# Moving the later forget-logit loads of a gated-attention and MLP-mixer kernel to the queue of its other loads, in the order of need

## The chip, the cores and the metric

The kernel runs on one core of a Trainium2 chip. The metric is device time in microseconds (us), lower is better. The planner inside the kernel, not the compiler, decides the order of instructions on each engine, so a small edit can change the order of many others. Engines: TensorE (PE) with its weight loads (PEld), VectorE (DVE), ScalarE (ACT), GpSimd (POOL) and SyncE (SP). POOL issues loads on the software queue, SP on the sync queue. A run counts as slow when it took over 1.5% longer than the fastest run of the same kernel; only the other, fast runs are compared.

## The reference, cut to what matters

```python
batch, n_heads, seq, head_dim = (4, 8, 768, 48)
f = 1.0 / (1.0 + np.exp(-f_logit))
for t in range(S):                                   # gated linear attention
    state = f[:, :, t, :, None] * state + einsum('bhd,bhe->bhde', k[:, :, t], v[:, :, t])
    y[:, :, t] = einsum('bhd,bhde->bhe', q[:, :, t], state)
x = y as (B, S, 384)
h = np.maximum(x.T @ w_tok1, 0.0) @ w_tok2           # token mixing, 768 -> 256 -> 768
u = x + h.T
out = u + np.maximum(u @ w_ch1, 0.0) @ w_ch2         # channel mixing, 384 -> 1536 -> 384
```

Inputs and output are float32. Each batch is cut into six chunks of 128 time steps. While a batch is mixed, the attention of the next one runs between its matmuls.

## The kernel before

Every load is a node of a plan: POOL, SP or DVE spends some time on it, then a made-up engine `Q` transfers it. The order of issue on each engine is all that the plan decides.

```python
    def load_f(b, c, key, at=0.0):                    # forget logits: sync queue, float32
        i = b % 2
        deps = [made.get(("lo", b - 2, c))]           # the buffer's last reader
        if b:
            def token(e):                             # holds the load back until DVE gets here
                nc.vector.memset(f_sb[i][0:1, c, 0, 0:1], 0.0)
            deps = [add({"DVE": 0.06}, token, key, deps, at=at)]
        def issue(e):
            nc.sync.dma_start(out=f_sb[i][:, c], in_=chunk_of(f_logit, b, c))
        n = add({"SP": 0.1}, issue, key, deps, at=at)
        made["f", b, c] = add({"Q": 1.1}, None, key, [n])

    def load_qkv(b, c, key, at=0.0):                  # software queue, cast to bfloat16
        ...
            made[name, b, c] = swdge(
                lambda e, dst=dst, src=src: nc.gpsimd.dma_start(out=dst[i][:, c], in_=chunk_of(src, b, c)), ...)

    def gates(b, c0, c1, key):                        # Exp, Ln -> Lhi, Ln, then Llo = f - Lhi
        ...
        o = add({"POOL": 0.85 * n} if b > 1 else {"DVE": 0.4 * n + 0.08},
                lambda e: on(e).tensor_tensor(lo, fb, hi, ALU.subtract), key, [g, h])
...
        xn = made["xn", b, c] = add(..., copy(e, x_nat[i][:, c, :], t["py"][:, 0:DM]))   # PSUM -> float32
        made["xb", b, c] = add(..., copy(e, x_bf[i][:, c, :], x_nat[i][:, c, :]))        # -> bfloat16
...
    for c in range(NCH):
        load_f(0, c, 0.1 * c)
        load_qkv(0, c, 0.1 * c)
    load_w("w_tok1", ...); load_w("w_tok2", ...); load_w("w_ch1", ...)
    for c in range(NCH):
        if c == W2:
            load_w("w_ch2", ...)
        load_f(1, c, 0.63 + 0.01 * c, at=24.0 + 2.0 * c + (6.0 if c >= W2 else 0.0))
        load_qkv(1, c, 0.63 + 0.01 * c)
    ...
                if b >= 1:
                    load_f(b + 1, c, b + 0.05 + 0.1 * c)       # no `at`: as soon as the buffer is free
                    load_qkv(b + 1, c, b + 0.05 + 0.1 * c)
```

`tok1`, `tok2`, `ch1`, `ch2` below are the matmuls with the four weights. Lhi is the logarithm of the forget gate (with its sign turned) in bfloat16, Llo what that rounding left over; attention needs both. x_bf is the attention's output in bfloat16, h1T the inner activation of token mixing.

## Time and profile before

| | before |
|---|---|
| median of 4 runs | 216.56 us (216.18 to 218.65) |
| span of the profiled run | 215.3 us |
| first tok2 / ch1 / ch2 matmul of batch 0 | 42.6 / 51.2 / 73.7 us |
| last packet of q/k/v of batches 0, 1, 2, 3 | 26.2 / 75.3 / 92.3 / 116.9 us |
| w_ch2 landed | 73.6 us |

Landings are from the packet records of the trace. From the page of the kernel before, busy time of each engine and the queues; a queue's line has packets, MB and the time of its packets as a share of the 16 DMA engines' span:

```profile
PE 182.8 (85%) x1768; PEld 112.8 (52%) x1768; DVE 134.7 (63%) x317; ACT 141.7 (66%) x315; POOL 77.5 (36%) x90
...
q0 software_dynamic: 77888, 10.23, 70.9%
q1 hardware_dynamic: 28416, 9.44, 25.1%
```

The busy times by stage, kernel before. Each line: stretch, its length, busy time of each engine (instructions), granted TensorE clock, DMA share (time of the packets over that of the 16 DMA engines; packets overlap, so it can exceed 1), GB/s:

```profile
0.00:20.00 20.00, 7.21 (x77) 4.28 (x78) 8.72 (x28) 11.44 (x25) 14.57 (x24) 1.00 1.61 133
20.00:40.00 20.00, 15.93 (x178) 10.28 (x177) 15.42 (x43) 14.90 (x35) 11.73 (x14) 1.00 1.63 173
40.00:60.00 20.00, 17.06 (x158) 9.81 (x159) 14.61 (x42) 15.35 (x38) 8.88 (x10) 0.83 1.75 136
60.00:80.00 20.00, 17.46 (x179) 10.94 (x178) 13.96 (x35) 13.89 (x35) 8.75 (x10) 0.91 1.71 156
80.00:110.00 30.00, 25.82 (x297) 15.93 (x296) 25.80 (x51) 23.05 (x49) 25.75 (x26) 0.94 1.73 125
```

PE is idle 16.9 us in the first 40 us. The chain of waits of the kernel before (start, length, what) shows why:

```profile
6.16 11.41 DMA v_sb_82<-in_v_dram
...
23.93 13.63 DMA w_ch_76<-in_moe_w_ch_dram
...
37.84 16.27 DMA k_sb_81<-in_k_dram
...
54.41 19.22 DMA w_ch_77<-in_moe_w_ch_dram
73.68 2.10 PE pm L452 x6
```

The chain goes from load to load until w_ch2 (w_ch_77) lands and lets PE start ch2. The issues on SP's queue (start, length, the load, buffer 84 for even batches, 85 for odd ones):

```profile
0.75 33.30 SPq L211 DMA_DIRECT2D f_sb_84<-in_f_logit_dram  x11
34.10 3.44 SPq L211 DMA_DIRECT2D f_sb_85<-in_f_logit_dram  x1
37.64 2.06 SPq L211 DMA_DIRECT2D f_sb_84<-in_f_logit_dram  x1
39.76 33.80 SPq L211 DMA_DIRECT2D f_sb_85<-in_f_logit_dram  x11
```

Buffer 84 gets six loads for batch 0 and six for batch 2, and all twelve are issued by 37.6 us. So five of the six loads of batch 2, which nothing reads before 79 us, were issued before the first load of batch 1.

### The profile page before, as it was taken

What the parts mean: (1) busy time and instruction counts of PE and PEld (TensorE: products, weight loads), DVE (VectorE), ACT (ScalarE), POOL (GpSimd) and SP (SyncE); (2) the same over time, 40 slices, a digit from 0 to 9 for tenths busy, and PEclk for the clock granted to TensorE, in tenths of its full rate; (3) what the DMA queues carried; (4) which work ended last, traced back from release to release, by engine and by line L of the source; (5) the groups of instructions that cost most, each with busy time, mean ns of one, the idle gap of its engine ahead of it and who ended that gap; (6) DMA issues with size and microseconds to landing.
All of it is one profiled execution on the core that took longest, in us unless ns stands there. A gap on an engine that the chain in (4) does not pass through costs nothing.

```text
span 215.3 us, 4558 instructions
## 1 busy us (share of the span) xinstructions
PE 182.8 (85%) x1768; PEld 112.8 (52%) x1768; DVE 134.7 (63%) x317; ACT 141.7 (66%) x315; POOL 77.5 (36%) x90
## 2 busy tenths in 40 slices
PE   0525789588999597978989999998999999899993
PEld 0313555354566264645555656665666665466661
DVE  4428795386999538798898544779566584620122
ACT  5646796576999267495999924478986442789200
POOL 8937960434543179998495300000000000000000
PEclk9999999976999889996999999999999999999999
DMA  7999999999999999999979002210000132000032
GB/s 114 146 135 139 152 204 188 134 135 135 137 151 184 146 139 182 113 79 139 133 66 75 3 35 74 76 38 3 0 3 0 37 106 82 2 3 0 0 142 81
DMA packets 106326, 19.96 MB, mean 93 GB/s; under 512 B 100288, under 2 KB 105920, under 8 KB 106304
## 3 DMA queue, kind: packets, MB, share of 16 engines
q0 software_dynamic: 77888, 10.23, 70.9%
q1 hardware_dynamic: 28416, 9.44, 25.1%
q8 instruction: 14, 0.23, 0.5%
q14 instruction: 8, 0.07, 0.1%
HBM read 25.17 MB, written 4.72 MB: 139 GB/s over the span
## 4 chain that ended last, share of the span: by engine, by line
PE 52%; DMA 28%; DVE 6%; ACT 5%; POOL 5%; issue 2%; DVEq 0%; POOLq 0%
PE pm L452 21%; PE pm L433 16%; DMA w_ch_77<-in_moe_w_ch_dram 9%; DMA k_sb_81<-in_k_dram 8%; DMA w_ch_76<-in_moe_w_ch_dram 6%; DMA v_sb_82<-in_v_dram 5%; PE pm L384 3%; POOL k_sb_80 L228 2%; PE pm L403 1%; DVE u_nat_118 L407 1%; POOL q_sb_78 L228 1%; POOL v_sb_82 L228 1%; PE pk L292 1%; PE pq L292 1%; ACT u_bf L189 1%
## 5 line engine op out<-in xcount | busy, mean ns | idle before, releaser
L452 PE MATMUL pm<-w_ch_77,zT 128*128 128x384 bf16 x288 | 53.3, 331 | 2.5 <-DMA w_ch_77<-in_moe_w_ch_dram 2.5
L433 PE MATMUL pm<-uT,w_ch_76 128*128 128x384 bf16 x288 | 53.0, 330 | 0.0
L195 ACT ACTIVATE zT<-pm 128x384 bf16<-128x384 f32 x78 | 37.9, 503 | 4.1 <-PE pm L433 3.8
L452 PEld LDWEIGHTS <-zT 128*128 128x128 bf16 x288 | 26.8, 99 | 19.4 <-DMA w_ch_77<-in_moe_w_ch_dram 2.6
L433 PEld LDWEIGHTS <-w_ch_76 128*128 128x128 bf16 x288 | 26.7, 98 | 16.1 <-issue 0.7
L461 DVE TENSOR_TENSOR out_sb_122<-u_nat_118,pm 128x384 f32<-128x384 f32 x6 | 3.3, 550 | 17.5 <-PE pm L452 17.4
L228 POOL DMA_DIRECT2D k_sb_80<-in_k_dram x12 | 10.7, 888 | 9.1 <-DMA w_ch_77<-in_moe_w_ch_dram 6.5
L228 POOL DMA_DIRECT2D k_sb_81<-in_k_dram x12 | 10.8, 898 | 8.7 <-DMA w_ch_76<-in_moe_w_ch_dram 5.3
L403 PE MATMUL pm<-h1T,w_tok_75 128*128 128x384 bf16 x48 | 11.9, 371 | 2.1 <-ACT uT L189 1.2
L228 POOL DMA_DIRECT2D v_sb_83<-in_v_dram x12 | 10.8, 903 | 5.7 <-DMA q_sb_79<-in_q_dram 4.2
L228 POOL DMA_DIRECT2D q_sb_79<-in_q_dram x12 | 10.9, 912 | 4.3 <-DMA k_sb_81<-in_k_dram 2.4
L228 POOL DMA_DIRECT2D q_sb_78<-in_q_dram x12 | 10.9, 906 | 3.7 <-DMA k_sb_80<-in_k_dram 1.3
L228 POOL DMA_DIRECT2D v_sb_82<-in_v_dram x12 | 10.7, 896 | 3.5 <-DMA q_sb_78<-in_q_dram 1.4
L197 DVE TENSOR_SCALAR zT<-pm 128x384 bf16<-128x384 f32 x18 | 9.6, 551 | 3.2 <-PE pm L433 3.0
L189 ACT COPY x_nat_112<-py 128x384 f32<-128x384 f32 x11 | 5.3, 478 | 9.3 <-PE py L352 8.5
L272 ACT ACTIVATE G_90<-pS 128x384 bf16<-128x384 f32 x12 | 6.0, 497 | 7.3 <-PE pS L266 7.3
L418 PE MATMUL pm<-ident,u_bf 128*128 128x128 bf16 x72 | 7.5, 223 | 2.1 <-DVE u_bf L191 0.6
L259 PE MATMUL pS<-Lhi_86,tri_bf 128*128 128x384 bf16 x12 | 5.0, 415 | 4.9 <-ACT Lhi_86 L243 4.9
L384 PEld LDWEIGHTS <-w_tok_74 128*128 128x128 bf16 x48 | 5.2, 114 | 7.4 <-issue 6.0
L272 ACT ACTIVATE G_91<-pS 128x384 bf16<-128x384 f32 x12 | 5.8, 488 | 4.9 <-PE pS L260 3.4
L189 ACT COPY x_nat_113<-py 128x384 f32<-128x384 f32 x9 | 4.4, 492 | 6.8 <-PE py L352 6.8
L407 DVE TENSOR_TENSOR u_nat_118<-x_nat_113,pm 128x384 f32<-128x384 f32 x12 | 6.1, 546 | 3.9 <-PE pm L403 3.9
(228 smaller groups left out, 422.4 us busy)
## 6 DMA issues: line engine op xcount, KB each, us to landing
f_sb_84<-in_f_logit_dram SPq DMA_DIRECT2D x12, 192.0 KB, 8.3
f_sb_85<-in_f_logit_dram SPq DMA_DIRECT2D x12, 192.0 KB, 9.0
out_dram<-out_sb_122 SPq DMA_DIRECT2D x12, 192.0 KB, 1.9
out_dram<-out_sb_123 SPq DMA_DIRECT2D x12, 192.0 KB, 2.0
q_sb_78<-in_q_dram POOLq DMA_DIRECT2D x12, 96.0 KB, 7.1
k_sb_80<-in_k_dram POOLq DMA_DIRECT2D x12, 96.0 KB, 6.7
v_sb_82<-in_v_dram POOLq DMA_DIRECT2D x12, 96.0 KB, 7.0
w_ch_76<-in_moe_w_ch_dram POOLq DMA_DIRECT2D x1, 1152.0 KB, 13.6
```

Of the source, the lines that this page charges most:

```text
L189: nc.scalar.copy(dst, src)
L195: nc.scalar.activation(dst, src, AF.Relu, bias=0.0, scale=1.0)
L197: nc.vector.tensor_scalar(dst, src, 0.0, None, ALU.max)
L228: lambda e, dst=dst, src=src: nc.gpsimd.dma_start(out=dst[i][:, c], in_=chunk_of(src, b, c)),
L259: nc.tensor.matmul(Sv, lhsT=tri_bf, rhs=Lhi[i][:, c, :, 0:D], start=True, stop=False)
L272: return lambda e: nc.scalar.activation(dst.rearrange("t h d -> t (h d)"), t["pS"][:, 0:DM], AF.Exp, bias=0.0, scale=scale)
L384: nc.tensor.matmul(t["p"][:, 0:DM], lhsT=w_tok1[:, kt, rt * 128:(rt + 1) * 128], rhs=x_bf[i][:, kt, :], start=(kt == 0), stop=(kt == NCH - 1))
L403: nc.tensor.matmul(t["p"][:, 0:DM], lhsT=w_tok2[:, kt, tt * 128:(tt + 1) * 128], rhs=h1T[:, kt, :], start=(kt == 0), stop=(kt == 1))
L407: u = made["u", b, tt] = add({"DVE": 0.47}, lambda e, tt=tt, t=t: nc.vector.tensor_tensor(u_nat[i][:, tt, :], x_nat[i][:, tt, :], t["p"][: ...
L418: nc.tensor.matmul(t["p"][:, m * 128:(m + 1) * 128], lhsT=u_bf[:, tt, m * 128:(m + 1) * 128], rhs=ident, start=True, stop=True)
L433: nc.tensor.matmul(t["p"][:, 0:384], lhsT=w_ch1[:, kt, cc * 128:(cc + 1) * 128], rhs=uT[:, kt, th * 384:(th + 1) * 384], start=(kt == 0), ...
L452: nc.tensor.matmul(t["p"][:, 0:DM], lhsT=zT[:, kt, tt * 128:(tt + 1) * 128], rhs=w_ch2[:, kt, :], start=(kt == 0), stop=(kt == NCC - 1))
```

## The change

The intent: loads of later batches off the sync queue, so that one queue carries all loads but the forget logits of batch 0, in the order in which they are needed; the first loads before the masks are built. With it came a re-tuning of the plan. The diff, cut to its core:

```diff
-    make_upper_triangular(nc, tri_bf, val=1.0, diag=True)
-    make_identity(nc, ident)
-    f_sb = two([128, NCH, H, D], FP32, "f_sb")
+    f_sb = two([128, H, NCH, D], FP32, "f_sb")
-    out_sb = two([128, DM], FP32, "out_sb")
+    out_sb = [st([128, DM], FP32, f"out_sb{n}") for n in range(NCH)]
...
+        if b == 0:
+            ... six loads on the sync queue, as before
+        else:
+            m = swdge(lambda e: nc.gpsimd.dma_start(out=f_sb[i], in_=src), key, 2.28, 5.9, 0.3,
+                      [made.get(("lo", b - 2, c)) for c in range(NCH)], at)
...
-        o = add({"POOL": 0.85 * n} if b > 1 else {"DVE": 0.4 * n + 0.08},
+        o = add({"POOL": 0.85 * n, "DVE": 0.4 * n + 0.08} if b > 1 else {"DVE": 0.4 * n + 0.08},
...
-        made["xb", b, c] = add(..., copy(e, x_bf[i][:, c, :], x_nat[i][:, c, :]), ...)
+        made["xb", b, c] = add(..., copy(e, x_bf[i][:, c, :], t["py"][:, 0:DM]), ...)
...
-    PACE = (34.0, 5.6)
+    PACE = (34.0, 5.0)
+    load_f(0, 0.0)
+    load_qkv(0, 0, 0.0)
+    def masks(e):
+        make_upper_triangular(nc, tri_bf, val=1.0, diag=True)
+        make_identity(nc, ident)
+    made["masks"] = add({"POOL": 1.4}, masks, 0.0)
+    ... q/k/v of batch 0, w_tok1, w_tok2
+    load_f(1, 0.615)
+    load_w("w_ch1", ...)
+    ... q/k/v of batch 1, w_ch2 before its last chunk
...
-            n = 2 if b else 1
+            n = 2
-                gates(b + 1, c, c + n, b + 0.9 + 0.15 * c)
+                gates(b + 1, c, c + n, b + 0.85 + LEAD[0] + LEAD[1] * c)
```

More of the change, by code (lines that the diff above doesn't have):

```diff
@@ L200, in chunk_of, with swdge, load_f @@
         return src[b].rearrange("h (c t) d -> t h c d", t=C)[:, :, c, :]
-    def load_f(b, c, key, at=0.0):
-        i = b % 2
-        deps = [made.get(("lo", b - 2, c))]
-        if b:
-            def token(e):
-                nc.vector.memset(f_sb[i][0:1, c, 0, 0:1], 0.0)
-            deps = [add({"DVE": 0.06}, token, key, deps, at=at)]
-        def issue(e):
-            nc.sync.dma_start(out=f_sb[i][:, c], in_=chunk_of(f_logit, b, c))
-        n = add({"SP": 0.1}, issue, key, deps, at=at)
-        made["f", b, c] = add({"Q": 1.1}, None, key, [n])
-    issued = []
-    def swdge(fn, key, cost, us, deps, at=0.0):
-        ring = [issued[-6]] if len(issued) >= 6 else []
+    issued = []
+    def swdge(fn, key, cost, us, units, deps, at=0.0):
+        room, ring = 6.5 - units, []
+        for m, u in reversed(issued):
+            room -= u
+            if room < 0:
+                ring = [m]
+                break
         n = add({"POOL": cost}, fn, key, list(deps) + ring, at=at)
         m = add({"Q": us}, None, key, [n])
-        issued.append(m)
+        issued.append((m, units))
         return m
+    def load_f(b, key, at=0.0):
+        i = b % 2
+        src = f_logit[b].rearrange("h (c t) d -> t h c d", t=C)
+        if b == 0:
+            for c in range(NCH):
+                n = add({"SP": 0.05}, lambda e, c=c: nc.sync.dma_start(out=f_sb[i][:, :, c, :], in_=src[:, :, c, :]),
+                        key, [])
+                made["f", b, c] = add({"Q": 1.1}, None, key + 0.06 * c, [n])
+        else:
+            m = swdge(lambda e: nc.gpsimd.dma_start(out=f_sb[i], in_=src), key, 2.28, 5.9, 0.3,
+                      [made.get(("lo", b - 2, c)) for c in range(NCH)], at)
+            for c in range(NCH):
+                made["f", b, c] = m
     def load_qkv(b, c, key, at=0.0):
@@ L228, in load_qkv, with load_w @@
                 lambda e, dst=dst, src=src: nc.gpsimd.dma_start(out=dst[i][:, c], in_=chunk_of(src, b, c)),
-                key, 0.89, 0.72, [made.get((u, b - 2, c)) for u in users], at)
-    def load_w(name, dst, src, key, us):
+                key, 0.89, 0.71, 1.0, [made.get((u, b - 2, c)) for u in users], at)
+    def load_w(name, dst, src, key, us, units):
         made[name] = swdge(
             lambda e: nc.gpsimd.dma_start(out=dst, in_=src.rearrange("(kt p) n -> p kt n", p=128)),
-            key, 0.85, us, [])
+            key, 0.85, us, units, [])
     def gates(b, c0, c1, key):
@@ L238, in gates @@
         cs = range(c0, c1)
-        fb, hi, lo = f_sb[i][:, c0:c1], Lhi[i][:, c0:c1, :, 0:D], Llo[i][:, c0:c1, :, 0:D]
+        fb = f_sb[i].rearrange("t h c d -> t c h d")[:, c0:c1]
+        hi, lo = Lhi[i][:, c0:c1, :, 0:D], Llo[i][:, c0:c1, :, 0:D]
         cost = 0.08 + 0.33 * n
@@ L268, in attention @@
                                     [made["lo", b, c], made.get(("qh", *p2)), made.get(("kh", *p2)),
-                                     made.get(("st", *p2))], bank="att", at=at)
+                                     made.get(("st", *p2)), made["masks"]], bank="att", at=at)
         def decay(dst, scale):
@@ L341, in diag @@
                 copy(e, state_bd[j][64:64 + D, :, D:2 * D], state[j][64:64 + D])
-            made["bd", b, c] = add({"DVE": 0.5, "ACT": 0.5}, diag, key + 0.02, [s_, made.get(("y", *p2))])
+            made["bd", b, c] = add({"DVE": 0.5, "ACT": 0.55}, diag, key + 0.02, [s_, made.get(("y", *p2))])
         def readout(e):
@@ L356, in attention @@
                                   ms + [made["v", b, c], made.get(("bd", b, c - 1)) if c else None], bank="att")
-        xn = made["xn", b, c] = add({"ACT": 0.38, "DVE": 0.47},
-                                    lambda e: copy(e, x_nat[i][:, c, :], t["py"][:, 0:DM]),
-                                    key + 0.03, [made.get(("u", b - 2, c))], frees=y)
-        made["xb", b, c] = add({"DVE": 0.28, "ACT": 0.4},
-                               lambda e: copy(e, x_bf[i][:, c, :], x_nat[i][:, c, :]),
-                               key + 0.03, [xn, made.get(("t1", b - 2))])
+        either = {"ACT": 0.38, "DVE": 0.47}
+        made["xb", b, c] = add(either, lambda e: copy(e, x_bf[i][:, c, :], t["py"][:, 0:DM]),
+                               key + 0.03, [made.get(("t1", b - 2))], frees=y)
+        made["xn", b, c] = add(either, lambda e: copy(e, x_nat[i][:, c, :], t["py"][:, 0:DM]),
+                               key + 0.03, [made.get(("u", b - 2, c))], frees=y)
     def mixing(b, key0, span):
@@ L408, in mixing @@
                 u_nat[i][:, tt, :], x_nat[i][:, tt, :], t["p"][:, 0:DM], ALU.add),
-                kk, [made.get(("o", b - 2, tt))], frees=n)
+                kk, [made["xn", b, tt], made.get(("o", b - 2, tt))], frees=n)
             ub = add({"DVE": 0.28, "ACT": 0.4},
@@ L459, in mixing @@
             made["c2", b, tt] = half
-            o = out_sb[tt % 2]
+            o = out_sb[tt]
             n = made["o", b, tt] = add({"DVE": 0.47}, lambda e, tt=tt, t=t, o=o: nc.vector.tensor_tensor(
                 o, u_nat[i][:, tt, :], t["p"][:, 0:DM], ALU.add),
-                kk, [half, made.get(("out", tt % 2))], frees=first)
+                kk, [half, made.get(("out", tt))], frees=first)
             s = add({"SP": 0.1}, lambda e, tt=tt, o=o: nc.sync.dma_start(out=out_b[tt], in_=o), kk, [n])
-            made["out", tt % 2] = add({"Q": 0.7}, None, kk, [s])
+            made["out", tt] = add({"Q": 0.7}, None, kk, [s])
     W2 = 5
-    PACE = (34.0, 5.6)
-    for c in range(NCH):
-        load_f(0, c, 0.1 * c)
+    LEAD = (-0.05, 0.13)
+    PACE = (34.0, 5.0)
[5 more added lines that the diff above has]
+    made["masks"] = add({"POOL": 1.4}, masks, 0.0)
+    for c in range(1, NCH):
         load_qkv(0, c, 0.1 * c)
-    load_w("w_tok1", w_tok1, moe_w_tok1, 0.60, 3.3)
-    load_w("w_tok2", w_tok2, moe_w_tok2, 0.61, 2.2)
-    load_w("w_ch1", w_ch1, moe_w_ch1, 0.62, 6.0)
+    load_w("w_tok1", w_tok1, moe_w_tok1, 0.60, 3.0, 0.75)
+    load_w("w_tok2", w_tok2, moe_w_tok2, 0.61, 2.2, 0.25)
+    load_f(1, 0.615)
+    load_w("w_ch1", w_ch1, moe_w_ch1, 0.62, 6.0, 0.4)
     for c in range(NCH):
         if c == W2:
-            load_w("w_ch2", w_ch2, moe_w_ch2, 0.63 + 0.01 * c, 6.0)
-        load_f(1, c, 0.63 + 0.01 * c, at=24.0 + 2.0 * c + (6.0 if c >= W2 else 0.0))
+            load_w("w_ch2", w_ch2, moe_w_ch2, 0.63 + 0.01 * c, 7.6, 1.5)
         load_qkv(1, c, 0.63 + 0.01 * c)
@@ L487 @@
                 if b >= 1:
-                    load_f(b + 1, c, b + 0.05 + 0.1 * c)
+                    if c == 0:
+                        load_f(b + 1, b + 0.05)
                     load_qkv(b + 1, c, b + 0.05 + 0.1 * c)
-            n = 2 if b else 1
+            n = 2
             for c in range(0, NCH, n):
-                gates(b + 1, c, c + n, b + 0.9 + 0.15 * c)
+                gates(b + 1, c, c + n, b + 0.85 + LEAD[0] + LEAD[1] * c)
                 for a in range(c, c + n):
-                    attention(b + 1, a, b + 1.05 + 0.15 * a, PACE[0] + PACE[1] * (NCH * b + a))
+                    attention(b + 1, a, b + 1.0 + LEAD[0] + LEAD[1] * a, PACE[0] + PACE[1] * (NCH * b + a))
         mixing(b, b + 1.0, 1.0)
```

## The prediction

> **What bounds the kernel now.** The page: span 215.3 us, TensorE (PE) busy 182.8 us (85%), no other engine over 66%. The table by stage shows two regimes. From 0 to 40 us (attention of batch 0) PE is busy 23.1 us; it waits for loads and for the ACT/DVE chain behind them. From 40 us PE is the bound, busy 159.7 of 175 us, with holes: 2.9 us in 40-50, 2.5 in 70-80, 3.6 in 80-100, about 1 at each later batch change, 4 at the end (last output). The chain of waits runs through loads until 73.7 us: v chunk 11.4 us, w_ch1 13.6, k of batch 1 16.3, w_ch2 19.2.
>
> **Why loads are late.** q, k, v are 96-byte packets on the software queue, forget logits 192-byte packets on the sync queue. Where both are loaded (10-15, 50-55 us) the DMA moves 135 GB/s; where the software queue is nearly alone (30-35, 65-70 us) 184 to 207. Counting packets: about 1.0 per ns with both, up to 1.5 alone. The Trainium skill, "DMA: Bandwidth & Descriptors", Rules for kernel authors, says that spreading over issuing engines does not help bandwidth; the trace agrees and goes further: it costs. Also, forget logits of batch 2 on the sync queue take their share ahead of w_ch2.
>
> **What the change does.**
> 1. Batches 1 to 3: eighteen sync-queue loads and their DVE tokens (59 ns each, negligible) become three software-queue loads of 6144 packets: 4 to 6 us each at the rates above (estimate), POOL issue some 2 us (estimate from 0.88 us per 1024 packets now); POOL is 36% busy.
> 2. Order of need: token weights, f(1), w_ch1, q/k/v(1), w_ch2 before the last chunk. I expect w_ch1 at 38-41 us (37.6 before; first used at 51, harmless) and w_ch2 at 60-64 instead of 73.6. That removes the 2.5 us wait at 71-73.7 and the ragged stretch after it (late chunks of batch 1, next token mixing only at 97). PE idle in 40-110 falls from about 12 to 5-6 us.
> 3. First q/k/v ahead of the masks: 1.3 us earlier; batch 0 ends about as much earlier.
> 4. x_bf straight from PSUM: about 0.5 us off the chain to each token mixing. Six output buffers: little. Gates in pairs for batch 1: about 0.2 us of ACT per merged activation.
>
> **Clock.** The records show four half-clock stretches of 3.4 us between 40 and 105 us, up to 6.8 us lost, each after holes in PE's work. The Trainium skill, "TensorE: Matmul & The Clock Gate", Part 1, says that an idle window halves the clock. Fewer holes should remove about two: 2-3.5 us.
>
> **Sum.** 216.9 - 1.5 (start) - 6 (holes, 40-110) - 2.5 (clock) = about 207 us. PE's work is unchanged and bounds the rest; the tail stays. Range 202 to 212.5. Faster by over 2%: 0.87; within 2%: 0.11; slower by over 2%: 0.02.
>
> **What will show it.** Right: no wait for w_ch2; it lands before 65 us; DMA moves 170 GB/s or more after 25 us; loads end well before 117 us; PE busy 178-183 us, idle after 40 us 8-10 us; one or two half-clock stretches. Wrong: GB/s near 135 with one queue (packets, not mixing, limit), or a large f load fills the queue and POOL stalls for many us, delaying q/k/v.
>
> **What would make it wrong.** The long f load makes attention of batch 1 late, so PE idles around 40 us; ACT and DVE (82-99% busy at 50-70 us) become the bound, so holes only change their releaser; half-clock stretches fall elsewhere.

## The result, and the profile after

The changed kernel took 203.44 us (median of 4 runs, 202.69 to 205.03) against 216.56. The ratio was 0.9385, 95% interval 0.930 to 0.947. Two later sets of runs gave 0.9343 and 0.9369. A ratio is the mean time of one kernel's fast runs over that of the other's of the same rounds, so it is not quite the ratio of the medians quoted. Where "points" are compared below, they are differences of such ratios.

| | before | after |
|---|---|---|
| span of the profiled run | 215.3 | 200.9 us |
| first tok2 / ch1 / ch2 of batch 0 | 42.6 / 51.2 / 73.7 | 37.6 / 47.1 / 69.8 us |
| first tok1 of batches 1, 2, 3 | 97.5 / 141.2 / 180.7 | 79.4 / 122.6 / 162.0 us |
| last q/k/v packet of batches 0, 1, 2, 3 | 26.2 / 75.3 / 92.3 / 116.9 | 22.6 / 58.6 / 79.7 / 101.0 us |
| w_ch1 / w_ch2 landed | 37.6 / 73.6 | 38.7 / 56.8 us |
| half-clock stretches of PE after 40 us, 3.41 us each | 4 | 1 |

The page of the kernel after:

```profile
PE 176.1 (88%) x1768; PEld 110.1 (55%) x1768; DVE 139.7 (70%) x306; ACT 135.1 (67%) x300; POOL 77.8 (39%) x89
...
q0 software_dynamic: 78800, 13.77, 88.4%
q1 hardware_dynamic: 9696, 5.90, 10.7%
```

Three loads of 1152 KB moved from q1 to q0, but q0's packets rose by only 912 while q1's fell by 18720. In the packet records each later batch of forget logits is 272 packets of 4224 bytes and 16 of 1920 bytes: 22 rows of 192 bytes are merged into one packet. The q/k/v loads still send one 96-byte packet for each row. So the change did two things to these loads at once: it moved them to another queue, and it merged their rows (288 packets for a batch instead of 6144). No run here separates the two. The busy times by stage, kernel after:

```profile
0.00:20.00 20.00, 9.37 (x105) 6.17 (x106) 12.37 (x34) 13.19 (x30) 17.79 (x27) 1.00 1.96 138
20.00:40.00 20.00, 14.92 (x176) 9.04 (x174) 18.18 (x39) 12.74 (x29) 10.92 (x12) 1.00 1.43 188
40.00:60.00 20.00, 17.03 (x198) 10.89 (x198) 18.67 (x42) 17.89 (x41) 17.32 (x19) 0.91 1.90 162
60.00:80.00 20.00, 19.74 (x214) 12.42 (x212) 15.80 (x34) 15.13 (x31) 14.91 (x16) 1.00 2.13 155
80.00:110.00 30.00, 29.28 (x336) 18.76 (x334) 29.12 (x63) 27.08 (x63) 16.14 (x18) 1.00 1.38 114
```

PE's idle time from 40 to 110 us fell from 9.7 to 4.0 us. Over the whole span its idle time fell by 7.7 us (32.4 to 24.7) and its busy time by 6.7 us, for the same matmuls. Up to 5.1 us of the latter is time no longer spent at half clock (three stretches of 3.41 us fewer); full clock was also first recorded at 28.2 us, not 35.9. The chain of waits, kernel after:

```profile
5.98 7.63 DMA k_sb_72<-in_k_dram
...
22.96 15.73 DMA w_ch_68<-in_moe_w_ch_dram
...
42.65 5.13 DMA v_sb_75<-in_v_dram
...
49.77 15.63 DMA f_sb_76<-in_f_logit_dram
...
66.83 4.88 DMA v_sb_74<-in_v_dram
```

The chain still follows loads, but w_ch2 is no longer a link. SP's queue in the kernel after carries only batch 0 until the outputs begin:

```profile
0.74 6.16 SPq L221 DMA_DIRECT2D f_sb_76<-in_f_logit_dram  x6
73.48 0.36 SPq L470 DMA_DIRECT2D out_dram<-out_sb_114  x1
```

POOL's issues in the kernel after, first load of batch 1's forget logits (buffer 77), then w_ch2 (w_ch_69), then batch 2's forget logits (buffer 76), at 49.8 us and no longer from 6.9 us on:

```profile
20.72 2.30 POOL L225 DMA_DIRECT2D f_sb_77<-in_f_logit_dram  x1
...
46.17 1.04 POOL L239 DMA_DIRECT2D w_ch_69<-in_moe_w_ch_dram  x1
...
49.77 2.29 POOL L225 DMA_DIRECT2D f_sb_76<-in_f_logit_dram  x1
```

### The profile page after: what moved, and what is told of

Its sections match the earlier page's. It is cut to its first block, busy times and chain, and to the rows that moved or that the text cites. A ratio compares the mean times of both kernels' runs of the same rounds, so it can differ in the third digit from the quotient of the medians.

```text
span 200.9 us, 4497 instructions
## 1 busy us (share of the span) xinstructions
PE 176.1 (88%) x1768; PEld 110.1 (55%) x1768; DVE 139.7 (70%) x306; ACT 135.1 (67%) x300; POOL 77.8 (39%) x89
## 2 busy tenths in 40 slices
DMA packets 88517, 19.95 MB, mean 99 GB/s; under 512 B 81616, under 2 KB 87296, under 8 KB 88496
## 4 chain that ended last, share of the span: by engine, by line
PE 36%; DMA 29%; POOL 14%; DVE 12%; issue 4%; ACT 4%; POOLq 0%; DVEq 0%
PE pm L458 16%; PE pm L439 12%; DMA w_ch_68<-in_moe_w_ch_dram 8%; DMA f_sb_76<-in_f_logit_dram 8%; DMA q_sb_71<-in_q_dram 4%; DMA k_sb_72<-in_k_dram 4%; DMA v_sb_75<-in_v_dram 3%; DVE zT L196 3%; DMA v_sb_74<-in_v_dram 2%; POOL f_sb_77 L225 2%; POOL k_sb_73 L234 2%; POOL q_sb_70 L234 2%; PE pm L390 2%; POOL k_sb_72 L234 2%; POOL v_sb_74 L234 2%
## 5 line engine op out<-in xcount | busy, mean ns | idle before, releaser
L458 PE MATMUL pm<-w_ch_69,zT 128*128 128x384 bf16 x288 | 51.6, 326 | 0.1
L439 PEld LDWEIGHTS <-w_ch_68 128*128 128x128 bf16 x288 | 26.6, 98 | 18.5 <-issue 2.9
L409 PE MATMUL pm<-h1T,w_tok_67 128*128 128x384 bf16 x48 | 11.0, 332 | 0.5 <-ACT h1T L194 0.4
L467 DVE TENSOR_TENSOR out_sb_114<-u_nat_110,pm 128x384 f32<-128x384 f32 x2 | 1.1, 554 | 14.0 <-PE pm L458 14.0
L188 ACT CAST x_bf_106<-py 128x384 bf16<-128x384 f32 x7 | 3.3, 477 | 10.6 <-PE py L359 9.5
L196 DVE TENSOR_SCALAR zT<-pm 128x384 bf16<-128x384 f32 x16 | 8.6, 550 | 1.4 <-PE pm L439 1.4
L190 DVE COPY x_nat_105<-py 128x384 f32<-128x384 f32 x10 | 5.6, 557 | 5.8 <-ACT x_bf_107 L188 5.8
L188 ACT CAST x_bf_107<-py 128x384 bf16<-128x384 f32 x11 | 5.3, 481 | 6.0 <-PE py L359 5.5
L188 ACT CAST qT_91<-pq 128x512 bf16<-128x512 f32 x11 | 6.6, 596 | 3.9 <-PE pq L299 3.7
L254 DVE TENSOR_TENSOR Llo_80<-f_sb_76,Lhi_78 128x384 bf16<-128x384 f32 (+1 forms) x9 | 6.1, 687 | 3.1 <-ACT f_sb_76 L252 3.1
L424 PEld LDWEIGHTS <-u_bf 128*128 128x128 bf16 x72 | 5.0, 97 | 5.2 <-issue 2.1
```

The costliest lines, as they stand in the source:

```text
L188: nc.scalar.copy(dst, src)
L190: on(e).tensor_copy(dst, src)
L196: nc.vector.tensor_scalar(dst, src, 0.0, None, ALU.max)
L409: nc.tensor.matmul(t["p"][:, 0:DM], lhsT=w_tok2[:, kt, tt * 128:(tt + 1) * 128], rhs=h1T[:, kt, :], start=(kt == 0), stop=(kt == 1))
L424: nc.tensor.matmul(t["p"][:, m * 128:(m + 1) * 128], lhsT=u_bf[:, tt, m * 128:(m + 1) * 128], rhs=ident, start=True, stop=True)
L439: nc.tensor.matmul(t["p"][:, 0:384], lhsT=w_ch1[:, kt, cc * 128:(cc + 1) * 128], rhs=uT[:, kt, th * 384:(th + 1) * 384], start=(kt == 0), ...
```

## The experiments

Theories at the start. Order theory: the early loads of far-off batches (2 and 3) delay what is needed now; any queue would do if the order is right. Queue theory: what costs is that two queues are loaded at once. Schedule theory (rival to both): the re-tuned plan brings the gain. Twelve kernels ran; all were correct. The kernel before ran at 218.05, 218.31 and 217.97 us, so times are compared by ratio only.

| run | median us | ratio to before | 95% interval |
|---|---|---|---|
| e1_loads_only | 209.41 | 0.9531 | 0.946 to 0.960 |
| e2_before_f_late | 216.44 | 0.9848 | 0.976 to 0.994 |
| e3_f_on_sync | 216.34 | 0.9916 | 0.986 to 0.997 |
| e4_masks_first | 206.97 | 0.9513 | 0.944 to 0.959 |
| e5_after_again | 204.33 | 0.9343 | 0.927 to 0.942 |
| e6_lo_pool | 205.26 | 0.9414 | 0.935 to 0.948 |
| e7_f_on_sync2 | 212.83 | 0.9750 | 0.969 to 0.981 |
| e8_loads_lo | 204.59 | 0.9352 | 0.928 to 0.943 |
| e9_after_control | 203.68 | 0.9369 | 0.932 to 0.942 |
| e10_masks_same_order | 204.61 | 0.9397 | 0.935 to 0.945 |
| e11_f_six_sw | 205.46 | 0.9412 | 0.936 to 0.946 |
| e12_n1_lo_dve | 206.04 | 0.9462 | 0.941 to 0.951 |

### e1_loads_only

The changed kernel with its whole re-tuning undone, so only the loads (and the masks' place) are new.

```diff
-        made["xb", ...] copy from t["py"];  out_sb six buffers;  n = 2;  LEAD, PACE = (34.0, 5.0)
+        made["xb", ...] copy from x_nat;    out_sb two buffers;  n = 2 if b else 1;  old keys, PACE = (34.0, 5.6)
-        o = add({"POOL": 0.85 * n, "DVE": 0.4 * n + 0.08} if b > 1 else ...
+        o = add({"POOL": 0.85 * n} if b > 1 else ...
```

> The new loads (later forget logits as one software-queue load each, need order, first loads ahead of the masks) with all of the old schedule: x_bf copied from x_nat, two output buffers, old keys and pace, batch 1 gates one chunk at a time. If the gain comes from the loads: 203 to 208 us, w_ch2 landing before 62 us, PE reaching token mixing of batch 0 (first tok2 matmul) at about 38 us. If it comes from the schedule changes (the rival): 212 us or more.

Measured: ratio 0.9531 from two fast runs of four (206.83 and 208.50 us; the other two, 210.31 and 210.92, count as slow, and the profiled run was one of them). The fast runs lie at the upper end of the 203 to 208 us expected of the loads: they bring most of the gain, but by these two runs not all of it. The slow profile gave a hint, no more: a DVE product took 3.56 us, not 0.35, beside two Llo subtractions on POOL (from 85.3 us).

### e2_before_f_late

The kernel before, with the loads of batches 2 and 3 held back by a planned time.

```diff
-                    load_f(b + 1, c, b + 0.05 + 0.1 * c)
+                    load_f(b + 1, c, b + 0.05 + 0.1 * c, at=60.0 if b == 1 else 85.0)
```

> The kernel before, with one thing changed: the forget logits of batches 2 and 3 are held back (planned from 60 and 85 us) on the same sync queue; in the kernel before they were issued as soon as their buffer was free, from 6 and 46 us. If the early loads of far-off batches are what slowed batch 0 and w_ch2 (order theory): 207 to 211 us, first tok2 matmul of batch 0 near 38 us instead of 42.6, w_ch2 landing before 66 us. If what costs is only that two queues are loaded at once, whatever is in them (queue theory): 213 us or more, first tok2 matmul still at 41 us or later.

Measured: 0.9848, from two fast runs (213.18 and 215.98 us); the profile was of a slow run, so its times of work are not used. The time is far from the 207 to 211 us of the order theory, and the verdict at 2% is unclear. But the packet records of that profile show what the edit did to the loads. q/k/v of batch 1 were complete at 59.0 us and w_ch2 at 58.4 (75.3 and 73.3 before, 58.6 and 56.5 after), so the order brought these loads forward nearly as far as the change did, on two queues. The forget logits came late instead: those of batch 1 at 53.1 us (57.5 before, 32.9 after), and those of batch 3, issued from 98.1 us behind outputs in SP's order, at 109.5 us (79.0 before). So e2 doesn't bound what a good order is worth in time.

### e3_f_on_sync

The changed kernel with the later forget logits back on the sync queue, gated by DVE memsets.

```diff
-            m = swdge(... one load of the batch ...)
+            gate = made["w_tok2"] if b == 1 else made["v", b - 1, NCH - 1]
+            for c in range(NCH):
+                tok = add({"DVE": 0.06}, token, key, [gate, made.get(("lo", b - 2, c))], at=at)
+                n = add({"SP": 0.05}, ... nc.sync.dma_start(out=f_sb[i][:, :, c, :], ...), key, [tok], at=at)
```

> The changed kernel, with the forget logits of batches 1 to 3 put back on the sync queue as six chunk loads each, but in the order of need (gated by a DVE token after the token weights, or after the last v of the batch before). Order theory: within 1.5 us of the changed kernel, 203 to 205 us. Queue theory: 208 us or more, with the DMA near 135 GB/s while both queues are loaded.

Measured: 0.9916. This doesn't test the queue theory, because the edit missed its aim. The memsets stood late in DVE's order, so the loads of batch 1's forget logits were issued only from 36.3 us and complete at 58.2, and a Llo subtraction of batch 2 in POOL's order waited 23.4 us with q/k/v loads behind it. Run e7 repeats it properly.

### e4_masks_first

```diff
-    load_f(0, 0.0); load_qkv(0, 0, 0.0); made["masks"] = add({"POOL": 1.4}, masks, 0.0)
+    made["masks"] = add({"POOL": 1.4}, masks, -1.0); load_f(0, 0.0); load_qkv(0, 0, 0.0)
```

> The changed kernel with the masks built ahead of the first loads, as before. If the start of the loads moves the end: 204 to 205 us (1 to 1.5 us slower), first tok2 matmul about 1 us later than 37.6. If the start is hidden: within 0.5 us of 203.4.

Measured: 0.9513, more than expected. A comparison of the built programs told why the number can't be used for the masks: the planner had moved 1460 of 3538 PE rows (instructions). Run e10 repeats it with the order held.

### e5_after_again

No edit.

> The changed kernel itself, as the measure for the others of this call: ratio to the kernel before 0.935 to 0.945.

Measured: 0.9343, just below the range. One of its four runs, the profiled one, took 569.89 us; it is left out as slow (see the end).

### e6_lo_pool

```diff
-        o = add({"POOL": 0.85 * n, "DVE": 0.4 * n + 0.08} if b > 1 else {"DVE": 0.4 * n + 0.08},
+        o = add({"POOL": 0.85 * n} if b > 1 else {"DVE": 0.4 * n + 0.08},
```

> The changed kernel with one line undone: the subtraction that makes Llo for batches 2 and 3 (a two-chunk tensor_tensor of 1.64 us on POOL) may run on POOL alone again, not on POOL or DVE. In the loads-only run two DVE products with both inputs in SBUF took 3.2 and 3.6 us in place of 0.35 beside two such subtractions on POOL, and TensorE waited 5.4 us for them. If that blocking is what the loads-only version lost: 2 to 7 us slower than the changed kernel, with DVE products over 1 us beside the POOL subtractions. If it was chance of that order: within 1 us.

Measured: 0.9414 beside 0.9343; the intervals overlap, and the medians differ by 0.9 us, which is within what the expectation calls chance of that order (the edit changed the plan's order as well). In the changed kernel this line is worth 0.7 points by the ratios, not told from zero. The expectation also misread e1: only the product of 3.56 us ran beside Llo subtractions; the one of 3.23 us (82.2 to 85.4 us) ran beside load issues on POOL.

### e7_f_on_sync2

The changed kernel with the later forget logits on the sync queue, gated by a POOL memset which stands in POOL's order where the loads belong (one place after w_ch1 for batch 1).

```diff
-            m = swdge(... one load of the batch ...)
+            tok = add({"POOL": 0.2}, token, key, [posted[-1]] + [made.get(("lo", b - 2, c)) for c in range(NCH)])
+            for c in range(NCH):
+                n = add({"SP": 0.05}, ... nc.sync.dma_start(out=f_sb[i][:, :, c, :], ...), key, [tok], at=at)
```

> The changed kernel with the later forget logits on the sync queue as six loads each, now issued at the right place of the order (a POOL memset after the loads that come ahead of them, which the earlier try did with DVE and got f of batch 1 only at 45 to 58 us). Order theory: within 1.5 us of the changed kernel. Queue theory: 3 us or more slower, with 135 to 140 GB/s while both queues are loaded and w_ch2 landing 3 us or more after 56.5.

Measured: 0.9750 beside 0.9343, so 4.1 of the 6.6 points are lost; part of that can be the plan's order, which the edit changed too (see e11). w_ch2 landed at 59.0 us, 2.2 later than in the changed kernel, less than the 3 us that I had set. The late one is the load that moved: batch 1's forget logits, issued from 22.0 us, were complete at 46.4 us, against 32.9 after. The stage from 40 to 60 us of this run:

```profile
40.00:60.00 20.00, 14.62 (x113) 8.36 (x112) 13.64 (x27) 14.12 (x31) 12.26 (x15) 0.62 1.84 156
```

PE is busy 14.6 us of 20 at a granted clock of 0.62 (17.03 at 0.91 in the changed kernel). ACT in this run, where the last part of a line is the idle time just before it and what ended it:

```profile
37.49 0.84 ACT L252 ACTIVATE f_sb<-f_sb 128x768 f32<-128x768 f32 x1 [4.75 <-DMA f_sb<-in_f_logit_dram]
38.24 0.46 ACT L188 CAST x_bf<-py 128x384 bf16<-128x384 f32 x1
...
42.33 0.84 ACT L252 ACTIVATE f_sb<-f_sb 128x768 f32<-128x768 f32 x1 [1.32 <-DMA f_sb<-in_f_logit_dram]
43.08 0.47 ACT L194 ACTIVATE h1T<-pm 128x384 bf16<-128x384 f32 x1
```

In this trace ACT takes its work in the order of the plan. Its Exp of batch 1 stands ahead of the x_bf and h1T of batch 0 that PE wants; while the logits are on their way, ACT stands still (8.7 us in three waits), and PE goes idle and drops to half clock from 38.2 to 55.2 us. The packet records say why the logits are late. From 26 to 32 us, beside w_ch1, the sync queue got 0.06 packets per ns while w_ch1 got 0.07: one 192-byte packet for each packet of 3072 bytes. The Trainium skill, "DMA: Bandwidth & Descriptors", Queues, rings and completion order, says that each DMA engine goes round robin between queues packet by packet; this trace agrees. Beside w_ch1's large packets the queue of small ones starved here.

### e8_loads_lo

Run e1 with the Llo line of the change put back in.

```diff
-        o = add({"POOL": 0.85 * n} if b > 1 else ...
+        o = add({"POOL": 0.85 * n, "DVE": 0.4 * n + 0.08} if b > 1 else ...
```

> The loads-only version plus the one line that lets Llo of batches 2 and 3 run on DVE: old x_bf copy, two output buffers, old keys and pace otherwise. If loads and this line are the whole gain: ratio to before 0.935 to 0.947. If the remaining schedule changes are needed: as loads-only, 0.950 or more.

Measured: 0.9352, as the changed kernel (0.9343). So new loads and this one line give the whole gain. The copy of x_bf from PSUM, six output buffers, pairs of gates for batch 1, new keys and pace together bring nothing that these runs can tell from zero. Against e1 the line is worth 1.8 points. The line also changes the plan (in the traces, 356 of 1768 matmuls stand at another place), so the blocking on DVE isn't separated from the new order.

What the line avoids is seen in a fast run: in the kernel before, a DVE product that otherwise takes 0.36 us (median),

```profile
83.18 1.71 DVE L335 TENSOR_TENSOR state_108<-state_108,gl_106 128x192 f32<-128x192 f32 x1 [0.47 <-ACT G_91 L272]
```

ran 1.71 us, just beside POOL's subtraction,

```profile
83.01 1.65 POOL L247 TENSOR_TENSOR Llo_88<-f_sb_84,Lhi_86 128x768 bf16<-128x768 f32 x1
```

The Trainium skill, "SBUF — State Buffer", Who interferes with whom, says that a DVE instruction with two SBUF inputs contends with a GpSimd instruction that reads SBUF, and that the later one is blocked until the first ends. The two lines agree: DVE's ends 0.23 us after POOL's. It is the only DVE product above 1 us in that trace, beside six subtractions on POOL, so the blocking itself cost DVE 1.35 us there, less than the 1.8 points (some 3.9 us). Two subtractions are left on POOL in the changed kernel; beside the one at 101.5 us DVE took 1.35 us for the same kind of product.

### e9_after_control

No edit.

> The changed kernel, as the measure of this call: ratio to the kernel before 0.933 to 0.942.

Measured: 0.9369.

### e10_masks_same_order

The masks are emitted at the top, and their node in the plan does nothing. The orders on PE, ACT and DVE are, row by row, those of the changed kernel.

```diff
+    make_upper_triangular(nc, tri_bf, val=1.0, diag=True)
+    make_identity(nc, ident)
...
-    made["masks"] = add({"POOL": 1.4}, masks, 0.0)
+    made["masks"] = add({"POOL": 1.4}, lambda e: None, 0.0)
```

> The changed kernel with the two masks built ahead of the first loads, and the order of every other instruction on every engine left as it is (the earlier masks-first run had let the planner reorder 1460 of 3538 TensorE rows, so it told nothing of the masks alone). If the 1.3 us of later first loads pass through to the end: 0.4 to 0.8% slower than the changed kernel, first tok2 matmul 0.7 us or more later than the control. If they are hidden behind the two loaded queues and the chain of batch 0: within 0.3%, first tok2 within 0.4 us. The 1.3% that the earlier run lost would then be the new order.

Measured: 0.9397 beside 0.9369; the intervals overlap. In the profiles the first load is issued 0.4 us later (1.65 for 1.26 us), the first tok1 is 0.8 us later than in the control, the first tok2 0.2 us, the last matmul 0.6 us. So the place of the masks is worth 0.3 points or so, not resolved by the times. The rest of what e4 lost would be the order, by this argument.

### e11_f_six_sw

```diff
-            m = swdge(... one load of the batch ..., 2.28, 5.9, 0.3, ...)
+            for c in range(NCH):
+                made["f", b, c] = swdge(
+                    lambda e, c=c: nc.gpsimd.dma_start(out=f_sb[i][:, :, c, :], in_=src[:, :, c, :]),
+                    key, 0.85, 1.0, 0.05, [made.get(("lo", b - 2, c))], at)
```

> The changed kernel with each later batch of forget logits as six software-queue loads at the same place of the order, not one. If what counts is the queue and the order: within 1% of the control. If the single transfer counts (POOL issue of 2.3 us against six times about 0.9; packets of 22 rows against single rows): 2% or more slower, with w_ch1 or q/k/v of batch 1 landing 2 us or more later.

Measured: 0.9412 beside 0.9369; the intervals overlap. Six loads took POOL 5.36 us to issue, against 2.30, but rows were merged here as well (packets of 4224 and 3840 bytes), and batch 1's logits were complete at 32.2 us. One transfer or six makes no difference that these runs can tell, though the plan's order differs here from the changed kernel's (870 of 1768 matmuls in the traces). This run has a further use: its orders on PE, ACT and DVE are, row by row, those of e7, with loads of the same shape, and POOL's other work has the same order too. What differs is the queue of these loads, and with it the merging of rows, and one place in POOL's order for each batch (for batch 1, before w_ch1 here and after it in e7). The ratios are 0.9412 against 0.9750, with intervals far apart. So 3.4 points hang on moving these loads to the software queue, with the order of all other work held. The stage of which e7's line was shown, in this run:

```profile
40.00:60.00 20.00, 18.31 (x201) 11.63 (x200) 18.17 (x39) 16.21 (x40) 15.99 (x19) 0.88 1.91 163
```

PE does 201 matmuls there against 113 in e7, in the same order.

### e12_n1_lo_dve

An attempt at a faster version.

```diff
-            n = 2
+            n = 2 if b else 1
-        o = add({"POOL": 0.85 * n, "DVE": 0.4 * n + 0.08} if b > 1 else {"DVE": 0.4 * n + 0.08},
+        o = add({"DVE": 0.4 * n + 0.08},
```

> A try at a faster version: the changed kernel with the gates of batch 1 one chunk at a time again (TensorE waited 1.6 us at 41 to 43 us for the first pair's Llo) and no Llo on POOL at all. If that wait is worth its 1.6 us and the POOL subtractions still cost something: 0.5 to 1.5% faster than the control. If the order of the rest decides: within 1%, either way.

Measured: 0.9462 beside 0.9369: about one point slower. Nothing that ran beats the changed kernel.

## Why the prediction was right or wrong, point by point

The time (203.44 us) lies in the range of 202 to 212.5, and the direction was right. The gain, 13.1 us by the medians, was underrated: 9.9 was forecast. That the loads would come earlier and w_ch2's wait would go was right; the start, the clock and the packet counts behind the sum were not. The terms of the sum:

- **"1.5 (start)" was too small.** tok2 of batch 0 began 5.0 us earlier. Up to there PE was idle 18.5 us before and 15.5 after, and busy 24.1 and 22.1 us with nearly the same matmuls (268 and 269). So some 3 us are waits, and 2 us are shorter matmuls, which belong to the clock term. How the 5.0 us divide is partly chance: the control e9, the same kernel, had 14.0 us idle and 24.2 busy. The masks, which I gave as the reason, account for 0.2 us (e10 against its control); the first load was issued 0.4 us earlier (1.25 for 1.65 us), not 1.3. The step that failed: I read the sync queue's load as forget logits "of batch 2 ... ahead of w_ch2", and missed that batch 2's loads were issued from 6.9 us on, against q/k/v of batch 0. The last q/k/v packet of batch 0 came at 26.2 us before and 22.6 after. It came at 23.7 in e10, where the masks are first, at 23.0 in e7, where the sync queue is used again but later, and at 22.8 in e2, where nothing else in the kernel before was edited. So 2.5 to 3.4 of the 3.6 us are due to batch 2's loads being gone from there. What shortened the rest of the path to tok2 was not separated.
- **"6 (holes, 40-110)": right in size.** Idle time there fell by 5.7 us. But I gave 12 falling to 5-6; it was 9.7 falling to 4.0, my sum of the stages being wrong, so it is partly luck that the difference fits. w_ch2 landed at 56.8 us, earlier than the 60 to 64 that I gave; its wait is gone. The packet records of e2 and e7 (w_ch2 complete at 58.4 and 58.7 us, against 56.5 after) show that most of this needs only the better order, not the one queue.
- **"2.5 (clock)": the term furthest off.** Three of four half-clock stretches went, not two, and PE's busy sum fell by 6.7 us, to 176.1, below the 178 to 183 that I named (in the control e9 it was 177.6). The Trainium skill, "TensorE: Matmul & The Clock Gate", Part 1, ties half clock to idle windows of about 3.4 us. The traces agree on the length: 3.41 us each, and five such lengths (17.07 us) in e7 where PE starved. They don't show that a whole window must be idle: in the 3.41 us ahead of each of the four stretches of the kernel before, PE was busy 1.15 to 2.21 us (ends of matmuls are modelled), and the longest gap there was 2.5 us.
- **Two queues cost: shown in part, and by another route than mine.** I read 135 against 184-207 GB/s. That comparison was unsound, because the faster windows held larger packets. With one queue, q/k/v alone still move only 122 to 133 GB/s (15-20, 45-50, 65-70 us after), so my sign "170 GB/s or more after 25 us" failed. The packet counts hold: before, from 40 to 60 us, 0.57 packets per ns on the software queue and 0.42 on the sync queue, 0.99 in sum; alone, the software queue moved 1.46 (18-24 us before, 14-18 us after). Packet rate, not GB/s, is what to compare there, but queue by queue: the sync queue alone, with packets of 192 bytes, moved 1.06 (97-102 us of e7), so by these rates the mix would reach about 1.26 (estimate), and 0.99 is a fifth below that. e7 and e11 show what the move is worth in time: 3.4 points. An obvious rival is the merging of rows, which came with it: whether one queue with unmerged rows, or merged rows on the sync queue, would have done the same was not tried.
- **"4 to 6 us each" for a later f load: too small, and on a wrong basis.** I counted 6144 packets for each; there were 288, most of 4224 bytes. So the change took some 17,800 packets off the DMA (106326 to 88517), which I didn't foresee. The transfers took 6.9 to 7.9 us by their packets; POOL's 2.3 us to issue one was right. POOL did wait for room in the queue behind them (4.7 us at 29 us), but the DMA had work throughout; what I feared there did no harm.
- **Missed: the Llo line.** I did not mention that subtractions may now run on DVE. e8 against e1 puts the line at 1.8 points with the old plan (another order of work, and two fast runs), e6 at 0.7 with the new, not told from zero.
- **x_bf from PSUM, "about 0.5 us off the chain to each token mixing"; six output buffers; gates in pairs:** nothing that e8 can tell from zero.
- **Right as given:** w_ch1 38 to 41 us (38.7), PE idle after 40 us 8-10 us (9.0: 160.9 us less 151.9 busy), one half-clock stretch, loads done at 101.0 us.

So of the 6.6 points (e5), 3.4 (e11 against e7, the order of other work held) to 4.1 (e5 against e7, the order changed too) come from the later logits on the software queue, with merged rows, in place of the sync queue. What arrived too late without it were these logits (batch 1's at 46.4 us in e7 and 53.1 in e2, against 32.9), not w_ch2. The rest is put down by elimination, since e8 leaves nothing else: no longer loading batches 2 and 3 ahead of need, and the Llo line. How these two share it stays open: e2, e1 and e6 each also changed the plan's order, e2 made other loads late, and e1 and e2 rest on two fast runs each.

## What to carry to other kernels

Two loaded queues share the DMA packet by packet, so a load of small packets on a second queue neither gets its share of bytes beside large packets nor leaves the other queue its rate: try the loads that compete on one queue, in order of need, look at whether their rows become larger packets there, and ask of each prefetch what it delays. A late load delays everything that the plan puts behind it on the engine that waits, here work of the batch before (8.7 us on ACT in e7). When a planner decides the order, hold the order fixed (a no-op in the plan's place) before crediting a part of a change: e4 and e10 differ by more than a point for the same idea.

## What the Trainium skill lacked or had wrong

- "DMA: Bandwidth & Descriptors", Rules for kernel authors, says that spreading DMAs over issuing engines doesn't help bandwidth. Here it cost packets: 0.99 per ns with two queues of small packets, where the software queue alone moved 1.46 and the sync queue alone 1.06. In bytes it was 136 GB/s against 141 and 204.
- The same page, SWDGE vs HWDGE vs iDMA, puts a packet at 4096 bytes or less preferably and at most 64 descriptors. The float32 loads on the software queue came as packets of 4224 bytes (22 rows of 192). The q/k/v loads, which cast to bfloat16, came as one 96-byte packet for each row in every run. The page doesn't say whether a cast stops the merging; no run here changes the cast alone.
- "TensorE: Matmul & The Clock Gate", Part 1, gives an idle window as the condition of half clock. Here PE was busy 1.15 to 2.21 us of the 3.41 us ahead of each half-clock stretch of the kernel before.
- No page that I read warns that the granted clock may have no record at first: the column shows 1.00 from 0 to 35.9 us of the kernel before, where four 128x128 matmuls of pq or pk took 0.59 to 0.63 us, and about 0.40 after the first record.
- No page that I read describes a whole run like one of the changed kernel: 569.89 us, with ch1 and ch2 matmuls of 882 and 895 ns in the mean (329 and 326 in the fast profile), while ACT and DVE took as long as usual (Exp, Ln and ReLU 509 ns in the mean, 516 in the fast profile). Its trace has no clock record at all, and the column shows 1.00 throughout. It came once, and its cause stays open.
